# Two token groups of the last FFN: second products four jobs behind instead of three, with a third place for the activation's parts

## The chip, the cores and the metric

One core of a Trainium2 chip runs the whole program as one launch. The time is device microseconds of that core; before the change it is 949.03 us, the median of three runs (946.15, 949.03, 952.19). All shapes are fixed, and all numbers are 32-bit floats.

## The reference

Attention comes first: 4 batches, 8 heads, 512 local tokens with a window of 32 and 32 global tokens, head size 64. Its result, 2176 tokens of 512 numbers, goes through two feed-forward layers (FFNs), each with a hidden layer of 2048:

```python
def _moe_ref(x, w_in, w_out):            # first FFN
    r = np.maximum(x @ w_in, 0.0)
    return (r * r) @ w_out

def _moe2_ref(x, w_in, w_out, a, b):     # second FFN
    h = x @ w_in
    h2 = h * h
    P = a[0] + a[1] * h + a[2] * h2 + a[3] * h2 * h
    Q = 1.0 + np.abs(b[0]) * np.abs(h) + np.abs(b[1]) * h2
    return (P / (Q + 1e-06)) @ w_out
```

The change lies wholly in the second FFN, in the last two of its six token groups.

## The kernel before, in words

**Jobs.** Both FFNs are cut into jobs (list `jobs`, L299 to L309). A job is one slice of 128 of the 2048 hidden columns for one group of tokens. The second FFN has six groups: five of 384 tokens and one of 256. The first four run alone, 16 jobs each. The last two (384 and 256 tokens) run together (L303): their jobs alternate, 384, 256, 384, 256, 32 jobs in all, numbers 140 to 171. The first of the second FFN's jobs is `N1` = 76; `NJ` is 172.

**What a job does.** Every 32-bit operand is kept as two parts, a rounded high part and the rest, and each product takes three matmuls: high by high, high by low and low by high.
- `do_h` (matmuls at L333): the first product h = x @ w_in, 12 matmuls, into one of two PSUM banks (`bank("S")`, taken in turn).
- `rat_a`, `rat_b`, `rat_c` (L365 to L393): the rational function. `rat_a` reads h from its bank: on ScalarE L369, L370, L371, on VectorE L372, L373, L374. `rat_b` is ScalarE L381, L382 (logarithm and exponential for the division), then VectorE L383, L384, L385. `rat_c` writes the parts of the result: the high part on ScalarE (L391), the low part on VectorE (L392). The parts go into a place that `h_slot` (L283) hands out; there are two places, in turn.
- `do_y` (matmuls at L413): the second product, parts @ w_out, 3 matmuls for each 128 tokens: 9 for a job of 384 tokens, 6 for one of 256. The ones with the high part come first, those with the low part last. It adds up over a group's 16 jobs in PSUM banks that the group holds from its first job to its last.

**Order.** The program is written out step by step (`manual_schedule`; every engine works through its own instructions in the order written). Step k (L445) writes, in this order: `do_h(k)`; splits of a coming group's x into parts (`x_split`, L312); the second products that are due, `do_y(k-3)`; then `rat_a(k)`, `rat_b(k-1)`, `rat_c(k-2)`; then evacuations of finished groups (L434 on ScalarE, and the transfer out, L435). So TensorE sees h(k), y(k-3), h(k+1), y(k-2), ..., ScalarE sees L369 to L371 of job k, L381 and L382 of job k-1, L391 of job k-2, and VectorE likewise. The lag of three is the number in L476 to L483.

**Places of x.** The parts of x lie in rows of the buffer `big0`, in five places of two rows (`x_free`, L262); two more places (`x_more`) lie elsewhere and hold the 256-token group's x. The parts that `rat_c` writes lie in `big1`. The weights of both groups are in SBUF before the merged jobs start.

Of the kernel before, what the change touches and what calls it, by code (L numbers as in the profile page):

```python
# [10 lines left out]
F32R = mybir.dt.float32r  # L11
# [12 lines left out]
def kernel(  # L24
# [23 lines left out]
    NF = DFF // 128  # L48
# [10 lines left out]
    NMAX = 384  # L59
# [6 lines left out]
    def bank(tag):  # L66
        i = turns[tag].pop(0)
        turns[tag].append(i)
        return ps.tile([128, 512], F32, tag=f"b{i}", name=tag)
# [162 lines left out]
    def cv_tick(left):  # L232

        cv["z"] += 1
        for it in line:
            it["age"] += 1
        if cv["z"] >= cv["per"] and len(todo) > left:
            cv["z"] = 0
            it = todo.pop()
            if it["mode"] == "both":  # L240
                w_back(it)
            else:
                it["age"], it["at"] = 0, cv["at"] if it["mode"] == "wide" else OS
                w_load(it)
                line.append(it)
        for nm in ORD:
            for it in line:
                if it["at"].get(nm) == it["age"]:
                    OPS[nm.replace("el", "l")](it)
        line[:] = [it for it in line if it["age"] < it["at"]["lo"]]  # L250

    def cv_idle():
        return not (todo or line)
# [3 lines left out]
    rows, turn = [], dict(xs=0, hl=0)  # L257

    def row(i, r, n):
        return rows[i][:, NMAX * r:NMAX * r + n]  # L260

    x_free = [0, 1, 2, 3, 4]  # L262
    x_more = {}

    def x_room(ph, gi):
        late = len(groups_of[1]) - gi if ph else 9
        return [i for i in x_free if (i < 5 if late in (2, 3) else i >= 5 if late == 1 else True)]

    def x_slot(ph, gi, n, z):
# [10 lines left out]
        x_free.remove(i)  # L280
        return i, [x[:, 0:n].bitcast(F32R) for x in pair]

    def h_slot(n):  # L283
        i = turn["hl"] = (turn["hl"] + 1) % 2
        return [row(1, 2 * i + z, n).bitcast(F32R) for z in range(2)], row(2, i, n)


    groups_of = [[], []]
# [11 lines left out]
    for ph in range(2):  # L300
# [3 lines left out]
        for run in runs:  # L304
            fs = groups_of[ph][run[0]][2]
            for f in fs:
                for gi in run:
                    t0, n, _, add = groups_of[ph][gi]
# [3 lines left out]
    def x_split(ph, gi, t0, n, k):  # L312
        i, (hi, lo) = x_slot(ph, gi, n, k)
        src = xT[:, k, t0:t0 + n]
        sc.copy(hi, src)  # L315
        ve.tensor_tensor(out=lo, in0=src, in1=hi.bitcast(F32), op=ALU.subtract)
        xs[ph, gi, k] = hi, lo, i
        if k == NK - 1 and groups_of[ph][gi][3]:
            sy.dma_start(xT[:, :, t0:t0 + n], park[:, :, t0:t0 + n])
# [3 lines left out]
    def do_h(j):  # L323
        ph, gi, t0, n, f, _, last, _ = jobs[j]
        w = wt[ph, f]
        h = bank("S")[:, 0:n]
        wk = [[w[:, s, 0, 128 * k:128 * k + 128] for s in range(2)] for k in range(NK)]
        x = [xs[ph, gi, k] for k in range(NK)]
        mm = [(k, s, 0) for k in range(NK) for s in range(2)] + [(k, 0, 1) for k in range(NK)]
        if last:  # L330
            mm = [(k, s, t) for k in range(NK) for s, t in ((0, 0), (1, 0), (0, 1))]
        for m, (k, s, t) in enumerate(mm):
            pe.matmul(h, wk[k][s], x[k][t], start=m == 0, stop=m == 3 * NK - 1)  # L333
        if last:
            x_free.extend(i for i in [xs.pop((ph, gi, k))[2] for k in range(NK)] if i is not None)
        hps[j] = h
# [51 lines left out]
    def rat_c(j):  # L388
        s, _ = mid.pop(j)
        (hi, lo), _ = h_slot(jobs[j][3])  # L390
        sc.copy(hi, s)  # L391
        ve.tensor_tensor(out=lo, in0=s, in1=hi.bitcast(F32), op=ALU.subtract)  # L392
        gs[j] = hi, lo  # L393
# [3 lines left out]
    def do_y(j):  # L397
        ph, gi, t0, n, f, st, sp, add = jobs[j]
        hi, lo = gs.pop(j)
        w = wt[ph, f]  # L400
        if st:
            yb[ph, gi] = [bank("y") for _ in range(NK if ph == 0 else n // 128)]
        y = yb[ph, gi]

        ms = range(len(y))
        for m, z in [(m, z) for m in ms for z in range(2)] + [(m, 2) for m in ms]:
            c = slice(128 * m, 128 * m + 128)
            if ph == 0:
                a, x = w[:, z % 2, 1, c], (hi, hi, lo)[z]
                pe.matmul(y[m][:, 0:n], a, x, start=st and z == 0, stop=sp and z == 2)  # L410
            else:
                a, x = (hi, hi, lo)[z][:, c], w[:, z % 2, 1]
                pe.matmul(y[m], a, x, start=st and z == 0, stop=sp and z == 2)  # L413

        def evac1(m):
            o = xT[:, m, t0:t0 + n]
            if add:
                ve.tensor_tensor(out=o, in0=y[m][:, 0:n], in1=o, op=ALU.add)
            else:
                (sc.copy if m % 2 else ve.tensor_copy)(o, y[m][:, 0:n])  # L420

        def evac():
            if ph == 0:
                for m in range(NK):
                    if j == N1 - 1 and m:
                        held.append(lambda m=m: evac1(m))
                    else:
                        evac1(m)
            else:
                for m in range(n // 128):  # L430

                    ks, c = ((slice(0, 2), 0), (slice(2, 4), 0), (slice(0, 4), 256))[m]
                    o = xT[:, ks, t0 + c:t0 + c + (128 if c else 256)]
                    sc.copy(o, y[m].rearrange("p (k t) -> p k t", t=o.shape[2]))  # L434
                    sy.dma_start(out[t0 + 128 * m:t0 + 128 * m + 128, :].rearrange("p (k t) -> p k t", t=o.shape[2]), o)  # L435

        if sp:
            outs.append(evac)

    NJ = len(jobs)  # L440
    N1 = sum(j[0] == 0 for j in jobs)
    NR = len(REST) * NF
    ys = []

    def step(k):  # L445
        last, late = False, []

        if k < NR + 3:
            ticks, stage = (6 - (k > 5) if len(todo) > LEFT[2] else 2), (2 if k < NF else 3)
        elif k < N1 - (NF - NPRE) + 3:  # L450
            ticks, stage = 2, 4
        else:
            ticks, stage = (0 if cv_idle() else 6), 5
        left = LEFT[stage]
        if k < NJ:
            ph, gi, t0, n, f, _, last, _ = jobs[k]
            while (ph, f, 1) not in done:
                cv_tick(left)
            do_h(k)
        if k == N1:  # L460
            wide_s.close()
            pools["t"] = ctx.enter_context(tc.tile_pool(name="tmp", bufs=2, side="right"))
        if k >= N1 and not x_more and cv_idle():
            for i in (5, 6):
                x_more[i] = [cv3.tile([128, 512], U32, tag="T", name="xm").bitcast(F32) for _ in range(2)]
                x_free.append(i)
        for d in (1, 4, 7, 10):
            if k + d < NJ and jobs[k + d][5]:
                for z in range(NK):
                    if jobs[k + d][:2] + (z,) not in xs and x_room(*jobs[k + d][:2]):  # L470
                        x_split(*jobs[k + d][:4], z)
                        if d > 1:
                            break


        lag = [2 if y < N1 else 3 for y in ys[:2]]  # L476
        if ys and ys[0] <= k - lag[0]:
            do_y(ys.pop(0))
            lag.pop(0)
        while ys and (ys[0] <= k - lag[0] or (last and lag[0] == 2 and ys[0] < k)):  # L480
            do_y(ys.pop(0))
            lag.pop(0)
            lag.append(2 if ys and ys[0] < N1 else 3)  # L483
        if k < NJ:
            if ph == 0:
                late = list(relu2(k, k < NF))
                ys.append(k)
        rat = [lambda op=op, d=d: op(k - d) for d, op in enumerate((rat_a, rat_b, rat_c)) if N1 <= k - d < NJ]
        for op in rat[::-1] if k < N1 + 3 else rat:
            op()  # L490
        if N1 <= k - 2 < NJ:
            ys.append(k - 2)
        while outs:
            outs.pop(0)()
        if held and k >= N1 + 6:
            held.pop(0)()

        for t in range(ticks):
            if late and t == 1:
                late.pop(0)()  # L500
            cv_tick(left)
        for f in late:
            f()
# [463 lines left out]
    cv.update(at=OL, per=3)  # L967
    pools["b"] = ctx.enter_context(tc.tile_pool(name="wrest", bufs=1))
    turns.update(y=[2, 5, 3, 6, 4, 7])
    for k in range(NJ + 3):  # L970
        step(k)


# [29 lines left out]
```

## Time and profile before

| | |
|---|---|
| median of the runs | 949.03 us (946.15 to 952.19) |
| profiled execution, its own time | 947.44 us |
| its span, first to last instruction | 945.6 us |
| mean granted TensorE clock | 0.989 of full speed |
| TensorE matmuls busy | 902.8 us, 95% |
| TensorE weight loads busy | 821.3 us, 87% |
| VectorE busy | 722.9 us, 76% |
| ScalarE busy | 617.6 us, 65% |

The profile is of one execution. A timeline gives runs of equal instructions of one engine: start, length, what they are, how many, and in brackets the idle time of the engine before them with what ended it. The length of matmuls is modelled and includes the time in which the last one drains, so the time that a run takes from the next is read from start to start. The chain of waits follows the work that ended last backwards: at each step to what released it.

### The profile page before, as it was taken

The page shows a single profiled execution, that of the slowest core. Times are in us where ns is not written, and L with a number is a line of the kernel's source. Part 1 is how long each engine was busy: PE and PEld are TensorE (multiplying, and loading weights), DVE is VectorE, ACT ScalarE, POOL GpSimd, SP SyncE. Part 2 cuts the span into 40 slices and gives each one's busy share as a digit, 9 for nine tenths or more (in the row PEclk, how much of TensorE's full clock was granted, in tenths as well). Part 3 has the DMA queues.
Part 4 walks back from the last instruction along what each step waited for, and adds up shares of the span by engine and source line. Part 5 has one row for each costly group of instructions (what it writes and reads, how often), then busy time and mean ns, then how long its engine had stood idle before and what let it go on. Part 6 is the DMA issues. An engine that isn't in the chain of part 4 may idle for free.

```text
span 945.6 us, 19429 instructions
## 1 busy us (share of the span) xinstructions
PE 902.8 (95%) x7440; PEld 821.3 (87%) x7440; DVE 722.9 (76%) x1731; ACT 617.6 (65%) x1323; POOL 57.2 (6%) x109
## 2 busy tenths in 40 slices
PE   7868899999999999999999989999999999999997
PEld 4647788988999999999999979989889899888885
DVE  3599886765468576677765579989989999888886
ACT  3566465664578555555454467887887788877776
POOL 5233122210000000000000000000000000000000
PEclk9898999999999999999999999999999999999999
DMA  9998788630455255363522530010010010000001
GB/s 187 193 207 166 176 211 198 174 99 24 113 157 166 78 178 175 105 221 125 167 71 98 175 115 1 1 34 0 1 34 1 1 34 1 9 25 1 1 1 56
DMA packets 104301, 89.45 MB, mean 95 GB/s; under 512 B 60176, under 2 KB 87312, under 8 KB 104208
## 3 DMA queue, kind: packets, MB, share of 16 engines
q1 hardware_dynamic: 104208, 88.21, 35.0%
q8 instruction: 58, 0.95, 0.4%
q14 instruction: 35, 0.29, 0.1%
HBM read 62.13 MB, written 19.14 MB: 86 GB/s over the span
## 4 chain that ended last, share of the span: by engine, by line
PE 77%; DVE 9%; ACT 6%; DMA 4%; SPq 1%; issue 1%; POOL 0%; ACTq 0%; DVEq 0%; POOLq 0%
PE S L333 31%; PE y L413 17%; PE y L410 15%; PE H L532 3%; PE Y L557 3%; PE S L752 2%; PE PV L846 1%; DMA S<-in_moe_w_in_dram 1%; DVE T L168 1%; PE tr L719 1%; ACT ts L370 1%; ACT tq L371 1%; PE T L806 1%; DVE T L173 1%; ACT big L369 1%
## 5 line engine op out<-in xcount | busy, mean ns | idle before, releaser
L333 PE MATMUL S<-big,w 128*128 128x384 f32 (+1 forms) x1728 | 319.8, 330 | 2.0 <-ACT big L315 1.1
L333 PEld LDWEIGHTS S<-big,w 128*128 128x128 f32 x1728 | 294.2, 188 | 8.6 <-DVE ts L373 1.6
L413 PE MATMUL y<-w,big 128*128 128x512 f32 x816 | 208.8, 398 | 6.8 <-ACT big L391 5.1
L413 PEld LDWEIGHTS y<-w,big 128*128 128x128 f32 x816 | 149.0, 188 | 42.4 <-ACT big L391 8.5
L410 PE MATMUL y<-big,w 128*128 128x384 f32 (+1 forms) x912 | 159.7, 324 | 0.6 <-DVE xT L420 0.4
L410 PEld LDWEIGHTS y<-big,w 128*128 128x128 f32 x912 | 149.2, 188 | 1.5 <-DVE xT L420 0.7
L369 ACT ACTIVATE big<-S 128x384 f32<-128x384 f32 x96 | 45.4, 473 | 82.9 <-PE S L333 81.0
L348 ACT ACTIVATE big<-S 128x384 f32<-128x384 f32 (+1 forms) x76 | 35.5, 467 | 82.1 <-PE S L333 82.1
L356 DVE TENSOR_TENSOR big<-big 128x384 f32<-128x384 f32 (+1 forms) x60 | 31.3, 521 | 71.1 <-ACT big L352 71.0
L372 DVE TENSOR_TENSOR ts<-ts,S 128x384 f32<-128x384 f32 x96 | 50.8, 529 | 34.2 <-ACT ts L370 34.2
L371 ACT ACTIVATE tq<-big,coef 128x384 f32<-128x384 f32 x96 | 66.0, 688 | 0.0
L370 ACT ACTIVATE ts<-S,coef 128x384 f32<-128x384 f32 x96 | 62.4, 651 | 0.0
L333 PE MATMUL S<-xm,w 128*128 128x256 f32 (+1 forms) x336 | 60.7, 305 | 0.0
L373 DVE SCALAR_TENSOR_TENSOR ts<-ts,coef,S 128x384 f32<-128x384 f32 x96 | 56.9, 593 | 3.4
L352 ACT ACTIVATE big<-big 128x384 fp32r<-128x384 f32 (+1 forms) x76 | 38.2, 503 | 28.6 <-PE y L410 28.1
L150 ACT ACTIVATE T<-S 128x512 f32<-128x512 f32 x64 | 42.7, 668 | 19.0 <-DMA S<-in_moe_w_in_dram 8.2
L385 DVE SCALAR_TENSOR_TENSOR ts<-tq,ts 128x384 f32<-128x384 f32 x96 | 51.4, 536 | 3.3
L333 PEld LDWEIGHTS S<-xm,w 128*128 128x128 f32 x336 | 51.2, 188 | 2.9
L557 PE MATMUL Y<-f,w 128*128 128x256 f32 x360 | 51.4, 293 | 0.0
L532 PE MATMUL H<-f,w 128*128 128x256 f32 x360 | 51.0, 292 | 0.0
L374 DVE TENSOR_TENSOR tq<-tq,big 128x384 f32<-128x384 f32 x96 | 50.8, 529 | 0.0
L392 DVE TENSOR_TENSOR big<-ts,big 128x384 fp32r<-128x384 f32 x96 | 50.7, 528 | 0.1
(131 smaller groups left out, 1306.1 us busy)
## 6 DMA issues: line engine op xcount, KB each, us to landing
S<-in_moe_w_out_dram SPq DMA_DIRECT2D x32, 512.0 KB, 4.4
S<-in_moe_w_in_dram SPq DMA_DIRECT2D x32, 256.0 KB, 4.5
S<-in_moe_w_in_dram SPq DMA_DIRECT2D x16, 512.0 KB, 4.6
scr<-T SPq DMA_DIRECT2D x24, 256.0 KB, 2.8
T<-scr SPq DMA_DIRECT2D x24, 256.0 KB, 2.7
both<-stg SPq DMA_DIRECT2D x10, 512.0 KB, 3.5
w<-both SPq DMA_DIRECT2D x10, 512.0 KB, 5.3
out_dram<-xT SPq DMA_DIRECT2D x17, 256.0 KB, 2.6
```

What stands on the lines that cost most here:

```text
L333: pe.matmul(h, wk[k][s], x[k][t], start=m == 0, stop=m == 3 * NK - 1)
L369: sc.activation(av, h, AF.Abs)
L370: sc.activation(s, h, AF.Identity, scale=coef[:, 3:4], bias=coef[:, 2:3])
L371: sc.activation(q, av, AF.Identity, scale=coef[:, 7:8], bias=coef[:, 6:7])
L372: ve.tensor_tensor(out=s, in0=s, in1=h, op=ALU.mult)
L373: ve.scalar_tensor_tensor(out=s, in0=s, scalar=coef[:, 1:2], in1=h, op0=ALU.add, op1=ALU.mult)
L374: ve.tensor_tensor(out=q, in0=q, in1=av, op=ALU.mult)
L385: ve.scalar_tensor_tensor(out=s, in0=q, scalar=2.0, in1=s, op0=ALU.subtract, op1=ALU.mult, reverse0=True)
L410: pe.matmul(y[m][:, 0:n], a, x, start=st and z == 0, stop=sp and z == 2)
L413: pe.matmul(y[m], a, x, start=st and z == 0, stop=sp and z == 2)
L532: pe.matmul(h, w[:, s, 0, 128 * k:128 * k + 128], fx[a, k][t], start=m == 0, stop=m == 3 * NK - 1)
L557: pe.matmul(fy[m // 2][:, NSUB * (m % 2):NSUB * (m % 2) + NSUB], w[:, z % 2, 1, 128 * m:128 * m + 128], (hi, hi, lo)[z], start=f == 0 and ...
```

## The change

The places for the parts become three once job 141 has been started: the one place of x that is free then (two rows of `big0`) is taken out of `x_free` and joins the two of `big1`. From job 140 on, a second product is due four steps after its first product, not three. The places are handed out in turn, so the place of job j is written again for job j+3. The loop over steps has one step more. The test that decides which second products are due is written in another way; for the jobs before 140 it gives the same order.

```diff
+    h_more = []
+
     def h_slot(n):
-        i = turn["hl"] = (turn["hl"] + 1) % 2
-        return [row(1, 2 * i + z, n).bitcast(F32R) for z in range(2)], row(2, i, n)
+        i = turn["hl"] = (turn["hl"] + 1) % (2 + len(h_more))
+        pair = h_more[i - 2] if i > 1 else [row(1, 2 * i + z, NMAX) for z in range(2)]
+        return [x[:, 0:n].bitcast(F32R) for x in pair], row(2, i % 2, n)
@@
+    NL = NJ - 2 * NF
+
+    def lag_of(y):
+        return 2 if y < N1 else 3 if y < NL else 4
+
@@ def step(k):
-        lag = [2 if y < N1 else 3 for y in ys[:2]]
-        if ys and ys[0] <= k - lag[0]:
+        if k == NL + 1:
+            i = x_room(1, len(groups_of[1]) - 2)[0]
+            x_free.remove(i)
+            h_more.append([row(0, 2 * i + z, NMAX) for z in range(2)])
+
+        while ys and (ys[0] <= k - lag_of(ys[0]) or (last and ys[0] < min(k, N1))):
             do_y(ys.pop(0))
-            lag.pop(0)
-        while ys and (ys[0] <= k - lag[0] or (last and lag[0] == 2 and ys[0] < k)):
-            do_y(ys.pop(0))
-            lag.pop(0)
-            lag.append(2 if ys and ys[0] < N1 else 3)
@@
-    for k in range(NJ + 3):
+    for k in range(NJ + 4):
         step(k)
```

## Rows read from the trace of the kernel before

**Rows 1.** Stretches: us, busy us per engine, granted clock, DMA share; alone, then merged.
```profile
680.00:700.00 20.00, 20.00 (x102) 17.96 (x101) 18.07 (x35) 16.17 (x32) 0.00 (x0) 1.00 0.13 40
840.46:931.49 91.03, 87.82 (x469) 76.06 (x469) 75.62 (x170) 67.22 (x145) 0.00 (x0) 1.00 0.00 1
```

**Rows 2.** Who waited for whom, TensorE, 816 to 940 us: total, times, longest.
```profile
PE y L413 <- ACT big L391: 3.7, 14, 0.3
PE y L413 <- DVE big L392: 1.2, 3, 0.7
```

**Rows 3.** The chain of waits through one pair of merged jobs: start, us, what.
```profile
850.45 2.14 PE S L333 x12
...
852.61 0.49 ACT big L369
...
854.26 0.41 ACT tr L381
...
855.20 0.41 ACT big L391
...
855.65 2.40 PE y L413 x9
```

**Rows 4.** TensorE's timeline, from job 143 on: start, us, what.
```profile
824.00 1.60 PE L333 MATMUL S<-xm,w 128*128 128x256 f32 x12
...
829.62 1.08 PE L413 MATMUL y<-w,big 128*128 128x512 f32 x4
831.04 0.73 PE L413 MATMUL y<-w,big 128*128 128x512 f32 x2 [0.34 <-DVE big L392]
831.61 1.58 PE L333 MATMUL S<-xm,w 128*128 128x256 f32 x12
833.03 2.27 PE L413 MATMUL y<-w,big 128*128 128x512 f32 x9
835.14 2.24 PE L333 MATMUL S<-big,w 128*128 128x384 f32 x12
837.22 1.55 PE L413 MATMUL y<-w,big 128*128 128x512 f32 x6
838.61 1.60 PE L333 MATMUL S<-xm,w 128*128 128x256 f32 x12
```

**Rows 5.** TensorE's timeline, the end.
```profile
931.49 2.40 PE L413 MATMUL y<-w,big 128*128 128x512 f32 x9 [0.27 <-ACT big L391]
934.16 1.20 PE L413 MATMUL y<-w,big 128*128 128x512 f32 x4 [0.27 <-ACT big L391]
936.03 4.23 PE L413 MATMUL y<-w,big 128*128 128x512 f32 x17 [0.68 <-DVE big L392]
```

**Rows 6.** VectorE's timeline, two merged steps at full wait: start, us, what.
```profile
846.11 0.55 DVE L372 TENSOR_TENSOR ts<-ts,S 128x384 f32<-128x384 f32 x1 [1.16 <-ACT ts L370]
...
852.12 0.42 DVE L392 TENSOR_TENSOR big<-ts,big 128x256 fp32r<-128x256 f32 x1
853.70 0.56 DVE L372 TENSOR_TENSOR ts<-ts,S 128x384 f32<-128x384 f32 x1 [1.16 <-ACT ts L370]
854.29 0.61 DVE L373 SCALAR_TENSOR_TENSOR ts<-ts,coef,S 128x384 f32<-128x384 f32 x1
```

**Rows 7.** VectorE's timeline, the step of a 256-token job without TensorE's wait.
```profile
831.49 0.61 DVE L373 SCALAR_TENSOR_TENSOR ts<-ts,coef,S 128x384 f32<-128x384 f32 x1
...
835.74 0.56 DVE L383 SCALAR_TENSOR_TENSOR tq<-tq,big 128x384 f32<-128x384 f32 x1 [0.33 <-ACT big L382]
...
837.34 0.42 DVE L392 TENSOR_TENSOR big<-ts,big 128x256 fp32r<-128x256 f32 x1
```

**Rows 8.** TensorE's timeline in a lone group.
```profile
754.32 2.25 PE L413 MATMUL y<-w,big 128*128 128x512 f32 x9
```

**Rows 9.** VectorE's timeline at the same place.
```profile
754.74 0.55 DVE L392 TENSOR_TENSOR big<-ts,big 128x384 fp32r<-128x384 f32 x1
```

**Rows 10.** ScalarE's timeline, the last evacuations.
```profile
938.43 2.71 ACT L434 COPY xT<-y 128x512 f32<-128x512 f32 x5 [0.77 <-PE y L413]
```

## The prediction

> **What bounds the kernel now.** Start with the stretches. In a lone group of 384 tokens TensorE's matmuls are busy for all of the 20 us, at the full clock level (granted 1.00, 2.4 GHz); in the merged jobs they are busy 87.82 of 91.03 us, at the same clock, with no transfer under way (DMA share 0.00), and VectorE (83%) and ScalarE (74%) have room [rows 1]. So TensorE is the engine that should be full, and only in the merged jobs is it not. Next, who it waits for: from 816 to 940 us it waits 14 times on ScalarE's L391 before a second product, and 3 times on VectorE's L392 [rows 2]. It never waits for a bank of h or for a weight.
>
> The chain of waits tells why [rows 3]. When a 384-token job's first product ends (850.45 + 2.14), ScalarE runs L369 to L371 of that job, L381 and L382 of the job before, and only then the L391 whose output the next-but-one run of TensorE needs: from 852.61 to 855.61, 3.0 us. L391 needs none of those five; it stands behind them in a queue worked in order. TensorE has 2.81 us to cover them: a 256-token y (837.22 to 838.61, 1.39) and a 256-token h (831.61 to 833.03, 1.42) [rows 4]. After a 256-token h the cover is y (2.11) and h (2.08) of 384 tokens, and there is no wait [rows 4]. So it happens once a pair.
>
> What it costs is read from start to start. A pair without it takes 838.61 - 831.61 = 7.00 us [rows 4]; twelve pairs with it take 91.03 us [rows 1], 7.59 each: 0.59 a pair.
>
> **A rule weighed.** The idle column gives only 0.27 a wait, and 3.7 + 1.2 = 4.9 us for the whole stretch [rows 2]. The Trainium skill (Perfetto Trace Analysis, Identifying the Most-Contended Engine) calls matmul busy time a bad measure of the room left, because matmuls are pipelined. The trace agrees: 0.59 from start to start against 0.27 of idle. By the idle column the sum below would be 947.44 - 4.9 = 942.5; by starts it is 938.3, and I go by starts.
>
> **The change, part by part.**
> *Lag of four.* TensorE's order becomes h384, y384, h256, y256. Between the step that writes a job's parts and its second product there is now one further h and y, at least 2.81 us [rows 4]; the L391 that was 0.59 late is over 2 us early. The h starts also become evenly spaced: 2.11 + 1.42 = 3.5 and 1.39 + 2.08 = 3.5 us, instead of 2.8 and 4.2. No matmul, activation or vector instruction is added or taken away; no transfer is issued or moved, so SP's and POOL's queues stay as they are.
>
> *What is late next: VectorE.* Its two steps of a pair run without a break from 846.11 to 852.54, 6.43 us [rows 6]; at evenly spaced steps add the 0.33 for which L383 waits for L382 [rows 7]. That is 6.76 against TensorE's 7.00, so it keeps up, by little. In the lone groups it ran at 18.07 of 20.00 us with TensorE full [rows 1]. Taken at nothing; if it did not hold, every 0.1 us over 7.00 costs 1.4 us in fourteen pairs.
>
> *Banks of h.* VectorE frees a bank with L373, which ends at 854.90, 2.3 us after its h [rows 3, 6]. The bank is used again after y, h, y: 2.11 + 1.42 + 1.39 = 4.9 us. Where the lag changes, step 143 has no second product, and h144 follows h143 at once, at 825.43 [rows 4]; its bank was filled by 821.9 and is free by 824.2. h146 comes at 832.4, and L373 of job 144 ended at 832.10 [rows 7]: tight, but free. Cost 0; at most the 2.1 us of the y left out, once.
>
> *Third place.* L391 of job j overwrites the parts of job j-3, whose second product stands one step earlier on TensorE, before the h for which ScalarE waits anyway at L369. Before, the same held for j-2. Cost 0. The place itself is free: the fourth lone group's x is last read by h139, before job 141.
>
> *The sum.* Before, job 143's h starts at 824.00 and the last 17 matmuls at 936.03 [rows 4, 5]; at 2.09 / 9 = 0.232 us each they end by start-to-start time at 939.98. The work from 824.00 on is sixteen pairs less two h384 and one h256: 16 × 7.00 - 5.58 = 106.4 us, so without any wait the end is 930.4. The difference is 9.6 us: thirteen waits of about 0.59 (7.5), the wait of 0.6 at 831.04 [rows 4], and 1.5 after the last h [rows 5].
>
> *The end.* After the last h (job 171) TensorE has y167 to y171. The low part of job 169 is done 4.73 us after that h (837.76 - 833.03) [rows 4, 7]; the two matmuls that need it are reached after 1.39 + 2.09 + 4 × 0.232 = 4.41. A wait of 0.3 costs 0.5, as 0.34 cost 0.6 at 831.04. Job 170's and 171's parts follow within a further step of 3.2 us (half of 6.43), by 7.9, when the last of TensorE's work, at 8.35 + 0.5, still has 0.9 to go. So 0.5 stays. The evacuations (five, 2.7 us [rows 10]) and the transfers out hang on the last second products as before and move with them. The extra step of the loop holds only y171.
>
> Sum: 9.6 - 0.5 = 9.1 us. From the profiled execution, 947.44 - 9.1 = 938.3. That execution is 1.6 us under the median of the runs, so for the median I say **939.9 us**, 0.96% less.
>
> **The rivals.**
> *Only the visible idle time comes back.* If the start-up of a run of matmuls after a new operand (0.59 - 0.27) stayed without a wait, 4.9 us would be won: 949.03 - 4.9 = 944.1. For it: the idle column. Against it: after waits of nothing, h and y follow each other in 2.08 to 2.11 us [rows 4]. 10%.
>
> *The bubble moves to h.* If places for h were what is short, TensorE would reach h earlier, wait there, and nothing would be won: 949.0. The Trainium skill (Perfetto Trace Analysis, Optimization Strategy) says that a gap that repeats can mean too little SBUF or PSUM for the next tile; here the gap ends with L391, and no wait for a bank shows. The h banks stay at two. Against it: 2.3 us of use in a 4.9 us turn. VectorE falling short by 0.6 a pair would give the same time. 5%.
>
> *Slower: a false wait through `big0`.* The third place shares its buffer with the x that the 384-token h reads. If the order were kept by buffer and not by rows, such an h would wait for the L392 written last into the place. It bites where a 256-token job holds the third place and a 384-token h comes next: h148, h154, h160, h166. L392 ends 4.73 us after the h before it [rows 4, 7], and the next h is due after 1.39: 3.3 us each, 13.4 in all, 4.3 more than is won: 953.3. Above 2.3 us a wait it is a loss. Against it: in a lone group VectorE writes one place of `big1` at 754.74 while y reads another from 754.32 to 756.41 [rows 8, 9]; order is kept by rows there. 4%.
>
> *It doesn't do what it says*: were no place of x left at job 141, the program could not be written. The group before holds four of the five until its last h, and the next takes four. 1%.
>
> **How the numbers follow.** The forecast has 80%: a gain of 8.5 to 9.6. A measurement of this kernel tells about 1% from no change, 9.5 us, and the forecast lies just inside, with runs that scatter by 3 us to each side: I give "faster by over 1%" 37%, "within 1%" 58% (it also holds the rivals), "slower by over 1%" 5%, for what I have not seen. The range goes from the fastest run less the whole 9.6 (936.5) to the first rival and a little over (945).
>
> **What would show it.** Right: after job 144 TensorE's pairs at 7.0 us, ScalarE's L391 no longer a releaser of y; L369 waiting for h twice a pair; one wait of some 0.3 us on L392 after the last h; its last matmul some 9 us earlier. Wrong: waits before h (L333) on L373 or L392, or pairs at 7.2 us and more with VectorE unbroken.

## The result, and the profile after

The changed kernel takes 937.73 us, the median of four runs (936.96 to 943.12), beside 948.95 (946.15 to 952.19) for the kernel before; the ratio, estimated from all the runs and not the quotient of the two medians, is 0.9893, with an interval of 0.9844 to 0.9942. Run again beside other kernels it took 941.69 (938.73 to 942.18) against 948.11, ratio 0.9921 (0.9895 to 0.9947). Both intervals hold the predicted 0.9904. The profiled execution is the slowest of its four: 943.12 us, span 941.3.

In the kernel after, lines from `h_slot` on are a few numbers higher: L333 is L336, L369 to L374 are L372 to L377, L381 to L385 are L384 to L388, L391 and L392 are L394 and L395, L413 is L416.

The stretch of the merged jobs, with the columns of [rows 1]:

```profile
859.00:929.00 70.00, 70.00 (x391) 63.25 (x391) 64.76 (x142) 57.20 (x121) 0.00 (x0) 1.00 0.00 1
```

TensorE is now full there, as in the lone groups; VectorE is at 93%. Who waited for whom from 816 to 940 us, as in [rows 2]:

```profile
ACT big L372 <- PE S L336: 11.1, 15, 1.7
ACT big L372 <- DVE ts L387: 5.2, 10, 0.5
DVE tq L386 <- ACT big L385: 4.3, 12, 0.4
...
PE y L416 <- DVE big L395: 0.7, 3, 0.3
```

L391's successor L394 holds up no second product any more, and TensorE's three waits left are 0.7 us in all; the first two of them (0.35 and 0.19) lie ahead of the merged jobs' second products and are in the kernel before as well (0.34 and 0.20). ScalarE waits for TensorE instead. Its ten waits "on L387" are most likely of the same kind, with VectorE's event the last one by the profile. In one of them L372 starts at 913.18. L387 ended at 913.16, but the 256-token h, which started at 911.56 with a modelled length of 1.58, ended at 913.14, and so L372 starts 0.04 us after its h, as where the profile names h (there 0.03: h from 907.38 for 2.25, L372 at 909.66).

TensorE's timeline from job 143 on, the answer to [rows 4]:

```profile
829.10 1.59 PE L336 MATMUL S<-xm,w 128*128 128x256 f32 x12
830.53 2.25 PE L336 MATMUL S<-big,w 128*128 128x384 f32 x12
832.61 2.25 PE L416 MATMUL y<-w,big 128*128 128x512 f32 x9
834.70 1.58 PE L336 MATMUL S<-xm,w 128*128 128x256 f32 x12
836.12 1.55 PE L416 MATMUL y<-w,big 128*128 128x512 f32 x6
837.51 2.25 PE L336 MATMUL S<-big,w 128*128 128x384 f32 x12
839.60 2.25 PE L416 MATMUL y<-w,big 128*128 128x512 f32 x9
841.69 1.58 PE L336 MATMUL S<-xm,w 128*128 128x256 f32 x12
```

Here the order h384, y384, h256, y256 is to be seen, and pairs of 6.99 us (834.70 to 841.69), instead of 7.59. At 829.10 and 830.53 two first products stand in a row, without a gap between them. How early the high part now is, from one 384-token job, its L394 and then the second product that reads it, two steps later:

```profile
856.27 0.50 ACT L394 CAST big<-ts 128x384 fp32r<-128x384 f32 x1
```

```profile
860.56 2.25 PE L416 MATMUL y<-w,big 128*128 128x512 f32 x9
```

L394 ends at 856.77, 3.8 us ahead of it. The end, the answer to [rows 5]:

```profile
925.53 1.58 PE L336 MATMUL S<-xm,w 128*128 128x256 f32 x12
926.95 4.59 PE L416 MATMUL y<-w,big 128*128 128x512 f32 x19
931.74 4.23 PE L416 MATMUL y<-w,big 128*128 128x512 f32 x17 [0.20 <-DVE big L395]
```

After the last h one wait is left, for job 169's low part. VectorE's step of a 256-token job, the answer to [rows 7]:

```profile
908.71 0.56 DVE L386 SCALAR_TENSOR_TENSOR tq<-tq,big 128x384 f32<-128x384 f32 x1 [0.37 <-ACT big L385]
...
910.30 0.42 DVE L395 TENSOR_TENSOR big<-ts,big 128x256 fp32r<-128x256 f32 x1
910.75 0.56 DVE L375 TENSOR_TENSOR ts<-ts,S 128x384 f32<-128x384 f32 x1
```

VectorE waits 0.37 a pair for ScalarE's exponential and then goes on almost without a break; it has no more to give than the 7% of the stretch.

**Where the time went.** Job 134 is the last whose step is the same in every kernel below. Its first product starts at 785.90 before and at 790.97 after; the last second product ends, by start-to-start time (last run of matmuls, 0.232 us each), at 939.97 and at 935.68. So the part with the change in it took 154.07 and 144.71 us: 9.36 less. The profiled execution after was 5.07 us later ahead of it, so that its own time fell by 4.32 only (947.44 - 943.12).

### The profile page after: what moved, and what is told of

Same layout as the page of the kernel before. It is cut to its first block, busy times and chain, and to the rows that moved or that the text cites. A ratio compares the mean times of both kernels' runs of the same rounds, so it can differ in the third digit from the quotient of the medians.

```text
span 941.3 us, 19428 instructions
## 1 busy us (share of the span) xinstructions
PE 902.3 (96%) x7440; PEld 826.2 (88%) x7440; DVE 727.9 (77%) x1731; ACT 618.3 (66%) x1323; POOL 58.9 (6%) x109
## 4 chain that ended last, share of the span: by engine, by line
PE 80%; DVE 10%; DMA 4%; SPq 2%; ACT 2%; issue 1%; ACTq 0%; DVEq 0%
PE S L336 34%; PE y L416 19%; PE y L413 15%; PE H L539 4%; PE Y L564 3%; DMA S<-in_moe_w_in_dram 1%; DVE T L168 1%; PE tr L726 1%; PE PV L853 1%; DVE s L765 1%; DVE T L173 1%; PE S L759 1%; SPq L133 1%; SPq L596 1%; DVE w L193 1%
## 5 line engine op out<-in xcount | busy, mean ns | idle before, releaser
L336 PE MATMUL S<-big,w 128*128 128x384 f32 (+1 forms) x1728 | 320.4, 331 | 2.0 <-ACT big L318 1.1
L336 PEld LDWEIGHTS S<-big,w 128*128 128x128 f32 x1728 | 294.7, 188 | 8.5 <-DVE ts L376 1.7
L416 PE MATMUL y<-w,big 128*128 128x512 f32 x816 | 206.3, 396 | 2.2 <-ACT big L394 1.4
L416 PEld LDWEIGHTS y<-w,big 128*128 128x128 f32 x816 | 150.4, 188 | 33.1 <-DVE big L395 4.2
L413 PE MATMUL y<-big,w 128*128 128x384 f32 (+1 forms) x912 | 160.4, 325 | 0.6 <-DVE xT L423 0.6
L413 PEld LDWEIGHTS y<-big,w 128*128 128x128 f32 x912 | 150.4, 188 | 1.0 <-DVE xT L423 0.9
L372 ACT ACTIVATE big<-S 128x384 f32<-128x384 f32 x96 | 45.5, 474 | 72.2 <-PE S L336 61.4
L374 ACT ACTIVATE tq<-big,coef 128x384 f32<-128x384 f32 x96 | 66.1, 688 | 0.0
L336 PE MATMUL S<-xm,w 128*128 128x256 f32 (+1 forms) x336 | 60.8, 305 | 0.0
L388 DVE SCALAR_TENSOR_TENSOR ts<-tq,ts 128x384 f32<-128x384 f32 x96 | 51.5, 536 | 3.3
L336 PEld LDWEIGHTS S<-xm,w 128*128 128x128 f32 x336 | 51.1, 188 | 2.9
L395 DVE TENSOR_TENSOR big<-ts,big 128x384 fp32r<-128x384 f32 x96 | 50.8, 529 | 0.1
L377 DVE TENSOR_TENSOR tq<-tq,big 128x384 f32<-128x384 f32 x96 | 50.8, 529 | 0.0
```

What stands on the lines that cost most here:

```text
L374: sc.activation(q, av, AF.Identity, scale=coef[:, 7:8], bias=coef[:, 6:7])
L377: ve.tensor_tensor(out=q, in0=q, in1=av, op=ALU.mult)
L388: ve.scalar_tensor_tensor(out=s, in0=q, scalar=2.0, in1=s, op0=ALU.subtract, op1=ALU.mult, reverse0=True)
```

## The experiments

The measure for all is that part, from the start of job 134's first product to the end of the last second product in the profiled execution, because it repeats better than the whole time: the changed kernel's second profile has 144.69. The ratios of the times of whole runs stand beside it.

| kernel | job 134 starts | end | part, us | against before | ratio of times (interval) |
|---|---|---|---|---|---|
| before | 785.90 | 939.97 | 154.07 | | |
| changed, first profile | 790.97 | 935.68 | 144.71 | -9.36 | 0.9893 (0.9844 to 0.9942) |
| changed, again | 790.06 | 934.75 | 144.69 | -9.38 | 0.9921 (0.9895 to 0.9947) |
| lag four, two places | 788.33 | 933.02 | 144.69 | -9.38 | 0.9931 (0.9904 to 0.9958) |
| third place, lag three | 785.14 | 939.15 | 154.01 | -0.06 | 1.0002 (0.9982 to 1.0022) |
| before, `rat_c` earlier (see there) | 790.31 | 938.8 | 148.5 | -5.6 | 0.9927 (0.9901 to 0.9953) |
| lag four from job 132, two places | 789.27 | 932.86 | 143.59 | -10.48 | 0.9895 (0.9870 to 0.9920) |
| the same, `rat_c` earlier | 783.84 | 927.54 | 143.70 | -10.37 | 0.9883 (0.9855 to 0.9912) |
| before, one more copy | 789.11 | 947.14 | 158.03 | +3.96 | 1.0053 (1.0035 to 1.0070) |
| changed, one more copy | 791.20 | 936.12 | 144.92 | -9.15 | 0.9915 (0.9885 to 0.9944) |

The ratios agree with the part within their intervals, but for the kernel with the lag of four and two places: its interval ends at 0.9904, where its part would give 0.9901.

The theory, called "queue": L391 was late because it stood behind five instructions in ScalarE's queue, and a second product four steps behind has enough cover. The chief rival, "place": the parts had too few places.

**The changed kernel again.** No edit.

> The changed kernel again, as the measure for the others on this chip. Theory (13 waits on L391 and the late end go away, nothing else moves): from job 143's first product to the end of the last second product 106.6 us as in the first profile, 9.4 us less than before; median of the runs 9 to 10 us under the kernel before, ratio 0.990. The first profiled execution had 5.1 us more ahead of job 143; the theory says that this part scatters from run to run and is not of the change, so here it should lie within some us of the kernel before, on either side. Rival (the change also alters what lies ahead of job 143): the same 5 us again.

The part is 144.69 us, the same to 0.02. It began 4.16 us later than in the profile of the kernel before, which alone would speak for the rival. But kernels whose program ahead of the merged jobs is that of the kernel before start it just as late (790.31 and 789.11 in the table), and one with the lag of four starts it earliest of all (783.84). So the 5 us are scatter between executions, not of the change.

**Lag of four, two places.** The edit is against the changed kernel.

```diff
-        if k == NL + 1:
-            i = x_room(1, len(groups_of[1]) - 2)[0]
-            x_free.remove(i)
-            h_more.append([row(0, 2 * i + z, NMAX) for z in range(2)])
```

> The lag of four with the two old places only. Theory 'queue': the wait came from L391's position behind five other ScalarE instructions, not from a lack of places; with two places L391 of job k-2 must wait for the second product of job k-4, which follows the first product of job k on TensorE and ends 2.1 us after it, while L391 comes up 2.6 to 3.0 us after it in ScalarE's queue: no wait, pairs of 6.99 us, the same time as the changed kernel within 1 us. Rival 'place': the third place is what lets the lag work; L391 waits for TensorE in every step, pairs go back towards 7.6 us, up to 9 us slower than the changed kernel.

The part is 144.69 us: the third place is worth nothing. The rows that decide are ScalarE's L394 of a 384-token step and TensorE's second product that it must not overtake:

```profile
853.61 0.50 ACT L394 CAST big<-ts 128x384 fp32r<-128x384 f32 x1
854.62 0.38 ACT L372 ACTIVATE big<-S 128x256 f32<-128x256 f32 x1 [0.52 <-PE S L336]
```

```profile
850.91 2.25 PE L416 MATMUL y<-w,big 128*128 128x512 f32 x9
```

With two places L394 overwrites the parts that this second product reads. The product hands over at 853.00 (the next run of matmuls starts there) and ends at 853.16 by its modelled length; L394 starts at 853.61 in its turn, with no idle time ahead of it.

**Third place, lag of three.** The edit is against the changed kernel.

```diff
-        return 2 if y < N1 else 3 if y < NL else 4
+        return 2 if y < N1 else 3
```

> The third place alone, with the lag of three. Theory 'queue': nothing changes, L391 stands in the same position in ScalarE's queue and second products wait for it as before: pairs of 7.59 us, ratio 1.00 to the kernel before. Rival 'place' (a gap that repeats is a lack of buffers): pairs of 7.0 us, 9 us faster.

```profile
839.72 2.39 PE L416 MATMUL y<-w,big 128*128 128x512 f32 x9 [0.26 <-ACT big L394]
...
930.67 2.39 PE L416 MATMUL y<-w,big 128*128 128x512 f32 x9 [0.26 <-ACT big L394]
```

Between these two lie twelve pairs: 90.95 us, 7.58 each, with the old wait in every one. "Place" has fallen in both directions.

**`rat_c` ahead of `rat_b`, lag of three, two places.** The edit is against the kernel before.

```diff
-        for op in rat[::-1] if k < N1 + 3 else rat:
+        for op in rat[::-1] if k < N1 + 3 else [rat[0], rat[2], rat[1]] if NJ - 2 * NF + 2 <= k < NJ else rat:
```

> The kernel before (lag three, two places) with one change of order in the merged jobs: in each step rat_c of job k-2 is written ahead of rat_b of job k-1, so that L391 stands behind three ScalarE instructions, not five, and L392 ahead of L383 to L385 on VectorE. Theory 'queue': L391 ends 0.92 us sooner (L381 0.41 and L382 0.51 of the 256-token job are behind it), which is more than the 0.59 that it was late: pairs of about 7.0 us, 12 to 13 waits gone, 7 to 8 us faster than before; the end is not helped as much as by the lag of four. Rival (the lag itself is needed, because TensorE has to start its run of matmuls with an operand long ready, or because VectorE falls behind with the new order): pairs stay above 7.4 us, under 3 us gained.

Pairs take 7.01 us, without any lag of four. From job 141's first product to job 171's the kernel before takes 113.78 us (815.85 to 929.63), this one 106.21 (820.27 to 926.48): 7.6 us are won there. But only about 5.6 are left at the end of the part, less than the 7 to 8 expected:

```profile
926.48 1.60 PE L333 MATMUL S<-xm,w 128*128 128x256 f32 x12
927.92 4.10 PE L413 MATMUL y<-w,big 128*128 128x512 f32 x15
933.69 5.30 PE L413 MATMUL y<-w,big 128*128 128x512 f32 x15 [1.67 <-ACT big L391]
```

In the last steps, which keep the old order, job 170's parts come late for a second product that is only three jobs behind. The lag of four covers this. The last fifteen matmuls then take 5.30 us; in the last kernel of this section fifteen take 3.76. Here 0.232 us for each does not hold, for the granted clock was lower while most of them ran. The stretch, with the columns of [rows 1]:

```profile
935.00:938.00 3.00, 3.00 (x9) 2.32 (x8) 0.18 (x1) 1.56 (x3) 0.00 (x0) 0.50 0.00 0
```

So of what is lost at the end some 1.5 us are the lower clock, and the table's end for this kernel is read from the last matmul (its start, 938.60, and 0.232); read in this way, the other kernels end 0.1 to 0.2 us later than in the table. That is one execution, the slowest of four (945.34, the others 940.95 to 942.38), and whether the clock fell in the others too is not known. By the medians of whole runs, 942.02 against 948.11, the kernel won 6.1 us.

**One more copy ahead of L391**, in the kernel before and, with the same edit, in the changed one. Its result is read by nobody.

```diff
+        if j >= NJ - 2 * NF and jobs[j][3] == NMAX:
+            sc.copy(rows[2][:, 768:1024], s[:, 0:256])
         sc.copy(hi, s)
```

> The kernel before with one more ScalarE copy (128 x 256, its result is not used) right ahead of L391 in each 384-token job of the merged ones. It adds ScalarE work to the queue position under suspicion. Theory 'queue': each of the 0.3 to 0.4 us that it takes is paid in full by TensorE: pairs of 7.9 to 8.0 us, 14 to 16 pairs, 4.5 to 6 us slower than before. Rival (TensorE's wait is set by something else and L391 only happens to end last): under 2 us.

> The changed kernel with the same additional copy. Theory: L391 now has over 2 us to spare and ScalarE room of 1.4 us a pair, so the copy costs nothing: pairs of 6.99 us, within 1 us of the changed kernel. Rival (ScalarE or VectorE is already the bound of the pair in the changed kernel, in step with TensorE by chance): 4 us and more.

In the kernel before, ScalarE's rows show what the copy costs, and TensorE's what it does:

```profile
859.26 0.39 ACT L392 COPY big<-ts 128x256 f32<-128x256 f32 x1
859.55 0.51 ACT L393 CAST big<-ts 128x384 fp32r<-128x384 f32 x1
```

```profile
844.41 2.37 PE L415 MATMUL y<-w,big 128*128 128x512 f32 x9 [0.57 <-ACT big L393]
...
938.76 2.37 PE L415 MATMUL y<-w,big 128*128 128x512 f32 x9 [0.57 <-ACT big L393]
```

From start to start the copy takes 0.29 us; a pair takes (938.76 - 844.41) / 12 = 7.86 us, 0.27 to 0.28 more than before. So ScalarE's queue is paid for one to one. The pair came out under the expected 7.9, and the part grew by 3.96 us, under the 4.5 expected, since I had counted the copy by its length in the profile (0.39) and not by its spacing. In the changed kernel the same copy costs 0.21 us in all, so ScalarE does not bound the pair there.

**Lag of four sooner**, from job 132 on, with two places. The edit is against the kernel with the lag of four and two places.

```diff
-        return 2 if y < N1 else 3 if y < NL else 4
+        return 2 if y < N1 else 3 if y < NL - 8 else 4
```

> Lag of four already from eight jobs ahead of the merged ones (job 132 on), two places. Theory: the two waits of the second products of jobs 137 and 138 on L392 (0.6 and 0.5 us, behind the four splits of x on VectorE) go as well, because each has one more job of cover; job 141's first product is then due later than the last split: 1.0 us less than the changed kernel. Rival: the wait moves to the first product of job 141, which needs the last split: no difference to the changed kernel.

The part is 143.59 us, 1.12 less than the changed kernel's. The step without a second product now falls into a lone group, where two first products stand together, and job 141's first product follows without a wait:

```profile
793.49 4.32 PE L336 MATMUL S<-big,w 128*128 128x384 f32 x24
...
816.51 1.58 PE L336 MATMUL S<-xm,w 128*128 128x256 f32 x12
```

**The same with `rat_c` earlier** (both edits above).

> As the kernel with the lag of four from job 132 on and two places, and rat_c ahead of rat_b in the merged steps. Theory: the one wait at the end (0.2 us idle, job 169's low part) goes too: 1.0 to 1.5 us less than the changed kernel, the best version, if small. Rival: VectorE, which has 0.2 us of room a pair, loses time between L385 and L392 in the new order, and pairs take over 7.05 us.

143.70 us: no better. The pairs kept 6.98 to 6.99 us, so the rival did not come true either; but the wait at the end only changed hands, from job 169's low part to the next job's high part:

```profile
924.06 3.76 PE L416 MATMUL y<-w,big 128*128 128x512 f32 x15 [0.30 <-ACT big L394]
```

## Why the prediction was right, point by point

- **The wait and its cause**: right. Three runs show it independently: the lag alone takes the wait away, a shorter queue takes it away in every pair (7.01 us, though this kernel loses time at the end), and a longer queue makes it longer by what it is longer. L391 was to be over 2 us early and is 3.8.
- **0.59 a pair, not the 0.27 of the idle column**: right. Pairs went from 7.59 to 6.99, where I had 7.00. Most of the 0.59 is L391 itself: in the kernel before, y starts 1.85 us after the h ahead of it (853.80 to 855.65) for 1.42 without a wait, 0.43 later, and then takes 2.23 us for 2.11. The first rival, 4.9 us, has fallen.
- **Banks of h**: right. Two first products in a row at 829.10 and 830.53, no wait before any first product, so the bubble did not move to h.
- **VectorE keeps up**: right, and as narrowly as said: 64.76 of 70.00 us, with 0.37 a pair of waiting for ScalarE, where I had 0.33.
- **Third place at cost 0**: right, but it is also worth 0, which the prediction did not see. It had the rows for it: a second product four behind ends 2.1 us after the step's first product, L391 comes 2.6 to 3.0 after it. No wait through `big0` appeared, so the rival on the slower side has fallen.
- **The end**: right in kind. I had a wait of 0.3 for 0.5 us; it was 0.20 for about 0.4 (from 925.53 to 935.68 are 10.15 us, the matmuls alone 1.42 + 8.35).
- **The sum**: 9.1 predicted, 9.36 and 9.38 measured between the same points of the traces; a pair of 6.99 for 7.00 and 0.4 for 0.5 at the end make up the difference. The median came out 2.2 us under the forecast in the first measurement and 1.8 over it in the second; the traces show scatter of this size ahead of the second FFN's second products, so how near the median came is in part luck. Whether the gain is just over or just under 1% these runs can't tell; by the traces it is 9.4 of 949, 0.99%.

## What to carry to other kernels

Where an engine works through its queue in order, a result that is long computed can still be late, because its last small copy stands behind work that waits for something newer. Count the queue ahead of it from the event that starts the step, and compare it with what the consumer has to do meanwhile; with jobs of two sizes in turn, do it for each step, since by the order of the steps a lag of an even number of jobs gives both the same cover and an odd one does not (here 2.81 and 4.19 us with three, 6.99 for both with four). Before paying for a buffer along with the lag, check if the old buffer's reader is already done when its writer comes up in the queue.

## What the runs showed of the hardware that was not expected

The part ahead of job 134 scattered by 7.4 us between executions (783.84 to 791.20) although its work is the same, while in the changed kernel's two profiles the part behind it repeated to 0.02 us. The difference is there by the second FFN's first second product, which starts at 552.23 in the earliest of them and at 559.75 in the latest. In the attention stage the granted TensorE clock differs between them. The stretch from 50 to 100 us in the earliest and the latest (columns as in [rows 1], clock third from the end):

```profile
50.00:100.00 50.00, 39.80 (x712) 31.96 (x711) 47.96 (x152) 34.37 (x90) 16.86 (x20) 0.96 0.95 202
```

```profile
50.00:100.00 50.00, 40.66 (x645) 32.95 (x644) 46.80 (x141) 31.80 (x86) 16.52 (x19) 0.83 0.86 182
```

With 0.96 of the clock granted TensorE got through 712 matmuls, with 0.83 through 645, and 202 against 182 GB/s were moved. Which of these causes the other no run here shows. For a change worth 1% that lies behind such a stage, a difference taken between two points of the traces behind it is the sharper measure.

The other surprise stands at the end of the kernel with `rat_c` earlier. TensorE had waited there for L391 for 1.67 us, and from 935 to 938 us the granted clock was 0.50 instead of 1.00 (1.2 instead of 2.4 GHz), and the last fifteen matmuls took some 1.5 us more than at the higher level. In the kernel before, where the longest wait at the end is 0.68 us, the clock stayed at 1.00:

```profile
936.03:939.63 3.60, 3.60 (x16) 2.92 (x16) 2.00 (x5) 1.82 (x5) 0.00 (x0) 1.00 0.00 0
```

That the wait brought the lower clock about is not shown; it is one execution. But before a stretch is priced by a spacing taken elsewhere, its granted clock has to be read.
